# Scores, mask, scale and row maximum: one VectorE operation per head in place of two per half of the heads

## The chip, the cores and the metric

The kernel runs on one core of one Trainium2 chip. Its engines work side by side, each through its own list of instructions in order: TensorE (PE in the profile, with PEld for its weight loads), VectorE (DVE), ScalarE (ACT), GpSimd (POOL) and SyncE (SP), which here issues nearly all DMAs. The metric is the device time of one execution in microseconds. Three runs of the kernel before gave 841.65, 842.85 and 843.45; the median is 842.85.

## The reference

Eight sequences of 576 tokens with eight heads of 64 pass through a causal attention with a window of 64 tokens, and then through a mixer with a token step and a channel step:

```python
scores = scale * np.matmul(q, k.transpose(0, 1, 3, 2))
rel = pos[:, None] - pos[None, :]
mask = (rel >= 0) & (rel < window)
scores = np.where(mask, scores, -1000000000.0)
scores = scores - np.max(scores, axis=-1, keepdims=True)
attn = np.exp(scores)
attn = attn / (np.sum(attn, axis=-1, keepdims=True) + 1e-09)
x = np.matmul(attn, v)                                  # then heads side by side: [8, 576, 512]
u = x + (np.maximum(xt @ w_tok1, 0.0) @ w_tok2).T       # xt is x with tokens last
out = u + np.maximum(u @ w_ch1, 0.0) @ w_ch2
```

All inputs are float32 but the mixer's weights, which arrive as float64 and are converted on the chip. Matrix products of the mixer use each operand as a high and a low part (hi, lo) and three products.

## The kernel before

**Tiles.** The tokens of each sequence are nine blocks of 64. An attention tile is two such blocks, 128 rows of queries, and there are 36 of them, i = 0 to 35. Since the window is 64 tokens, a block of 64 queries meets 128 keys: its own block and the one before. So the scores of a tile are, for each of the eight heads, 128 rows by 128 keys. The heads come in two halves, u = 0 and u = 1 (head g = 2h + u, h = 0 to 3), and each half has one PSUM buffer of 128 x 512, called s, written by `qk` (L295).

**Softmax.** `softmax(i, u)` works on one half. For tiles 0 to 6 (N_PE is 7) the mask has been added by TensorE, and VectorE reduces the maximum straight from PSUM (L309, L310). For tiles 7 to 35 VectorE first multiplies the scores by the scale and adds the mask over the whole half, 512 elements, into a tile e in SBUF (L312), and then reduces e to the negated maximum of each of the four heads, four columns of the tile nm (L315). `softmax_exp` then takes the exponential of each head on ScalarE with that column as its bias, and sums it at the same time (L323, two instructions in the profile).

**After the softmax.** `pt_transpose` turns e on TensorE (L330, tile pp) and ScalarE copies it back (L332, pt). `av` multiplies with the values (L342, tile xp). `recip` adds 1e-9 to the sums and inverts them on VectorE (L350, L351, tile ri), and `norm` multiplies xp with that into x (L356). `split_x` makes the high part on ScalarE (L101, xhi) and the low part on GpSimd (L104, xlo). `tok1` (L387) multiplies xhi and xlo into h, `finish_h` and `finish_h_low` apply the ReLU and split it (L398, L407), and `tok2` makes one piece of u at a time: x is transposed into the PSUM tile up (L428), the second token product is added (L435), and ScalarE copies it out (L440).

**Conversion jobs.** Between these steps the float64 weights are converted on VectorE: `to_f32_a` (L204, L206, L207) and `to_f32_b` (L216, L218, L219), then an addition on GpSimd (L221), a copy on ScalarE and a subtraction on GpSimd (L101, L104). Whether a tile has such a job is written in the table JOBS.

**Order.** The order of each engine's instructions is the order in which the program calls these functions; nothing reorders it. One turn i of the loop (L497) gives, for the stage from tile 7 on: the transposes of tile i; `softmax(i + 1, 0)`; `recip(i)`; finished weight jobs and `split_x`; `softmax_exp(i + 1, 0)`; one piece of u; the first part of a conversion; `softmax(i + 1, 1)`; `tok1`; `softmax_exp(i + 1, 1)`; the second part of the conversion; `av(i)` and `norm`; the ReLU's low part; `qk(i + 2)`; and another piece of u. The score buffers have two slots, so `qk(i + 2)` needs the buffers of tile i + 1, which `softmax(i + 1, u)` frees. The tile e has four slots, nm three.

**Masks.** At the start GpSimd fills two masks of 128 x 128 (L168 to L173) with 0 and NEG, and ScalarE writes a second form of each, maskr, for the TensorE path, multiplied to NEG_PE (L174).

After the attention stage come the channel products (L651, L659, L871), which the change does not touch.

Of the kernel before, what the change touches and what calls it, by code (L numbers as in the profile page):

```python
# [15 lines left out]
AF = mybir.ActivationFunctionType  # L16
ALU = mybir.AluOpType
AX = mybir.AxisListType
# [4 lines left out]
P = 128  # L23
# [24 lines left out]
N_PE, N_EARLY = 7, 4  # L48
# [9 lines left out]

HOME = {"m1": "c2", "m6": "c3", "m7": "c4", "m5": "c5", "m2": "c6", "m4": "c0", "m3": "c1"}
SLOT, NSLOT = NPROD * 2 * P, 3  # L60
NEG = -1.0e9

NEG_PE = -2.0 ** 33

F64_LOW = 2.0 ** -15
F64_HIGH = struct.unpack("<f", struct.pack("<I", 0x47EFFFFF))[0]
# [7 lines left out]
def tile_blocks(i):  # L74

    p, t = divmod(i, TPP)
    if t == 4:
        return (2 * p, 8), (2 * p + 1, 8)
    b, t = (2 * p, t) if t < 4 else (2 * p + 1, t - 5)
    return (b, t), (b, t + 4)  # L80
# [3 lines left out]
def mixer_kernel(ctx: ExitStack, tc: tile.TileContext, qh, kh, vh, wt1, wt2, wc1, wc2, out):  # L84
    nc = tc.nc
    scale = 1.0 / math.sqrt(D)
# [36 lines left out]
    with ExitStack() as actx:  # L123
# [4 lines left out]
        mask = [pa.tile([P, P], F32, name=f"mask{m}") for m in range(2)]  # L128
# [21 lines left out]
        maskr = [pa.tile([P, P], F32R, name=f"maskr{m}") for m in range(2)]  # L150
# [13 lines left out]
        for m in (1, 0):  # L164
            nc.gpsimd.memset(mask[m], 0.0)
            for half in range(2):
                mh = mask[m][half * BLK:(half + 1) * BLK]
                nc.gpsimd.affine_select(out=mh, in_=mh, compare_op=ALU.is_ge, fill=NEG,  # L168
                                        base=-1, pattern=[[1, P]], channel_multiplier=-1)
                nc.gpsimd.affine_select(out=mh, in_=mh, compare_op=ALU.is_ge, fill=NEG,  # L170
                                        base=BLK, pattern=[[-1, P]], channel_multiplier=1)
            if m == 1:
                nc.gpsimd.memset(mask[1][0:BLK, 0:BLK], NEG)  # L173
            nc.scalar.activation(maskr[m], mask[m], AF.Copy, scale=NEG_PE / NEG)  # L174

        for c in range(2):
            nc.gpsimd.tensor_copy(swapped[:, c * BLK:(c + 1) * BLK], ident[:, (1 - c) * BLK:(2 - c) * BLK])
# [89 lines left out]
        s_ps, e_sb, st = {}, {}, {}  # L267
# [31 lines left out]
        def softmax(i, u):  # L299
            if u == 0:  # L300
                st[i] = (pa.tile([P, H], F32, name=f"nm{i}", tag="nm", bufs=3),
                         pa.tile([P, H], F32, name=f"sum{i}", tag="sum", bufs=3))
            nm, sm = st[i]
            mk = mask[1 if tile_blocks(i)[0][1] == 0 else 0]
            e = pa.tile([P, 4, P], F32, name=f"e{i}_{u}", tag="e", bufs=4)
            e_sb[i, u] = e
            nmu = nm.rearrange("p (j u) -> p j u", u=2)[:, :, u]
            if i < N_PE:
                nc.vector.tensor_reduce(out=nmu, in_=s_ps[i, u], axis=AX.X, op=ALU.max, negate=True)  # L309
                nc.vector.tensor_scalar_mul(nmu, nmu, scale)  # L310
                return
            nc.vector.scalar_tensor_tensor(  # L312
                out=e, in0=s_ps.pop((i, u)), scalar=scale,
                in1=mk.unsqueeze(1).to_broadcast([P, 4, P]), op0=ALU.mult, op1=ALU.add)
            nc.vector.tensor_reduce(out=nmu, in_=e, axis=AX.X, op=ALU.max, negate=True)  # L315

        def softmax_exp(i, u):
            e = e_sb[i, u]
            nm, sm = st[i]
            src, by = (s_ps.pop((i, u)), scale) if i < N_PE else (e, 1.0)  # L320
            for h in range(4):
                g = 2 * h + u
                nc.scalar.activation(e[:, h], src[:, h], AF.Exp, bias=nm[:, g:g + 1], scale=by,  # L323
                                     accum_out=sm[:, g:g + 1])
# [167 lines left out]
        for i in range(TOK1_FROM, NT + 1):  # L492
            m = min(n + (1 if i < TOK1_SLOW else 2), i)
# [3 lines left out]
        for i in range(-1, NT + 1):  # L497
# [18 lines left out]
            if i + 1 < NT:  # L516
                softmax(i + 1, 0)
# [11 lines left out]
            if i + 1 < NT:  # L529
                softmax_exp(i + 1, 0)  # L530
# [7 lines left out]
            if i + 1 < NT:  # L538
                softmax(i + 1, 1)
# [3 lines left out]
            if i < N_PE - 1:  # L543
                softmax_exp(i + 1, 1)
                while to_finish:
                    job_finish()
            for n in tok1_plan.get(i, ()):
                tok1(n)
            if N_PE - 1 <= i < NT - 1:
                softmax_exp(i + 1, 1)  # L550
# [29 lines left out]
    with ExitStack() as bctx:  # L580
# [89 lines left out]
        def new_op(name, ct):  # L670
            tag, bufs = OP_TAGS[ct]
            return ps.tile([P, CHUNK], F32, name=f"op{name}_{ct}", tag=tag, bufs=bufs)
# [13 lines left out]
        u = ul.pop(0)  # L686
# [12 lines left out]
        for ct in range(NCT):  # L699
# [3 lines left out]
            op = new_op("0", ct)  # L703
# [84 lines left out]
        for j in range(1, N_PLAIN):  # L788
            u, last = ul.pop(j), j == N_PLAIN - 1
# [4 lines left out]
            for half in range(2):  # L794
                g = []
# [33 lines left out]
                for ct in range(NCT):  # L829
                    op = new_op(f"{j}_{half}", ct)  # L830
# [141 lines left out]
```

## Time and profile before

| what | value |
|---|---|
| median of 3 runs | 842.85 us (841.65 to 843.45) |
| the profiled execution | 843.08 us |
| its span, first to last instruction | 841.3 us |
| mean granted TensorE clock | 0.993 |
| L312, mask and scale, 128x512 | 58 times, 39.2 us, mean 676 ns |
| L315, negated maximum, 128x512 to 128x4 | 58 times, 39.8 us, mean 686 ns |
| L323, exponential, 128x128 | 232 times, 90.5 us, mean 398 ns |

Times are microseconds unless marked ns. In a row of a group the fields are line, engine, operation, output <- input, shapes, count, then the busy time and the mean duration of one, then the idle time of the engine just before them and what ended it. In a row in order of time the first two fields are the start, counted from the start of the span, and the duration. In a waits row stand who waited, for whom, microseconds in total, times, and the longest. In a row of a stretch stand its length, the busy time and number of instructions of PE, PEld, DVE, ACT and POOL, the granted TensorE clock, the busy share of the DMA engines and GB/s.

### The profile page before, as it was taken

To read this page: it belongs to the slowest core of one execution; us is meant where nothing else is said; L and a number is where in the kernel's file an instruction comes from. 1 tells how busy PE (TensorE), PEld (TensorE's weight loads), DVE (VectorE), ACT (ScalarE), POOL (GpSimd) and SP (SyncE) were. 2 spreads that over 40 slices of the span, in tenths; PEclk is the share of its full clock that TensorE was granted. 3 is DMA by queue.
4 is the path that set the end of the run, shared out by engine and by line. 5 is a ranking of instruction groups with operands and counts; after the bars stand their busy time and mean duration, and the time that the engine had idled before them with its cause. 6 is when DMAs were issued, how large, how long until landed. Compare 5 with 4: busy or idle time off the path is not lost.

```text
span 841.3 us, 14830 instructions
## 1 busy us (share of the span) xinstructions
PE 820.7 (98%) x5878; PEld 681.4 (81%) x5878; DVE 529.1 (63%) x940; ACT 336.6 (40%) x1017; POOL 104.6 (12%) x110
## 2 busy tenths in 40 slices
PE   8989999999999999999999999999999999999998
PEld 5668888888879878888888888878888878888886
DVE  5889988888884795666425535367635367625252
ACT  6778889888885441213203211024202033202020
POOL 4433434343332000000000000000000000000000
PEclk9999999999999999999999999999999999999999
DMA  9657687677644546744413642324542424542002
GB/s 329 210 202 250 206 253 242 218 246 249 206 134 151 195 121 187 209 139 135 141 73 111 246 194 87 138 88 138 187 188 88 138 91 169 171 170 88 1 1 100
DMA packets 71621, 136.49 MB, mean 162 GB/s; under 512 B 7040, under 2 KB 41856, under 8 KB 69632
## 3 DMA queue, kind: packets, MB, share of 16 engines
q1 hardware_dynamic: 69440, 133.71, 46.8%
q10 hardware_dynamic: 2112, 1.84, 0.7%
q8 instruction: 46, 0.75, 0.4%
q14 instruction: 23, 0.19, 0.1%
HBM read 104.66 MB, written 30.87 MB: 161 GB/s over the span
## 4 chain that ended last, share of the span: by engine, by line
PE 69%; DVE 23%; issue 3%; ACT 3%; DMA 1%; SPq 0%; POOL 0%; POOLq 0%; DVEq 0%; ACTq 0%
PE gp L871 19%; PE op L659 11%; PE gp L651 8%; PE op_4a L659 4%; PE op_2b L659 4%; PE op_2a L659 4%; PE op_0b L659 4%; PE op_0a L659 4%; PE op_4b L659 4%; DVE nm L315 3%; DVE e L312 2%; PE up L435 2%; PE h L387 2%; DVE x L356 2%; DVE r L219 2%
## 5 line engine op out<-in xcount | busy, mean ns | idle before, releaser
L871 PE MATMUL gp<-m,w1hi 128*128 128x512 f32 x504 | 155.4, 389 | 0.7 <-DVE x L879 0.7
L871 PEld LDWEIGHTS gp<-m,w1hi 128*128 128x128 f32 x504 | 94.4, 188 | 21.2 <-DVE x L879 1.5
L871 PE MATMUL gp<-m,w1lo 128*128 128x512 f32 x252 | 98.1, 389 | 0.0
L323 ACT ACTIVATE e<-e,nm 128x128 f32<-128x128 f32 x232 | 90.5, 398 | 18.1 <-DVE nm L315 17.6
L638 ACT ACTIVATE ghi<-x 128x512 fp32r<-128x512 f32 x54 | 34.2, 632 | 119.9 <-DVE x L881 68.3
L875 ACT COPY x<-gp 128x512 f32<-128x512 f32 x18 | 10.4, 577 | 143.8 <-PE gp L871 143.8
L639 DVE SCALAR_TENSOR_TENSOR glo<-x,ghi 128x512 fp32r<-128x512 f32 x54 | 37.4, 693 | 38.1 <-ACT ghi L638 38.1
L638 ACT ACTIVATE ghi<-gp 128x512 fp32r<-128x512 f32 x50 | 29.8, 596 | 70.5 <-PE gp L651 70.4
L651 PE MATMUL gp<-ulo,w1hi 128*128 128x512 f32 x144 | 56.0, 389 | 0.0
L651 PE MATMUL gp<-uhi,w1hi 128*128 128x512 f32 x144 | 56.0, 389 | 0.0
L651 PE MATMUL gp<-uhi,w1lo 128*128 128x512 f32 x144 | 56.0, 389 | 0.0
L871 PEld LDWEIGHTS gp<-m,w1lo 128*128 128x128 f32 x252 | 47.3, 188 | 9.7
L342 PEld LDWEIGHTS xp<-v,pt 128*64 128x64 f32 x1152 | 38.2, 142 | 15.0 <-issue 7.0
L639 DVE SCALAR_TENSOR_TENSOR glo<-gp,ghi 128x512 fp32r<-128x512 f32 x50 | 34.4, 687 | 24.7 <-ACT ghi L638 24.6
L659 PE MATMUL op<-ghi,w2hi 128*128 128x512 f32 x128 | 49.8, 389 | 0.0
L659 PE MATMUL op<-ghi,w2lo 128*128 128x512 f32 x128 | 49.8, 389 | 0.0
L659 PE MATMUL op<-glo,w2hi 128*128 128x512 f32 x128 | 49.8, 389 | 0.0
L104 POOL TENSOR_TENSOR xlo<-x,xhi 128x512 fp32r<-128x512 f32 x32 | 41.3, 1290 | 40.3 <-ACT xhi L101 39.9
L342 PE MATMUL xp<-v,pt 128*64 128x64 f32 x1152 | 43.2, 230 | 2.1 <-ACT t1hi L101 1.9
L323 ACT ACTIVATION_READ_ACCUMULATOR e<-e,nm 128x1 f32 x232 | 45.0, 194 | 0.0
L435 PE MATMUL up<-t2hi,hhi 128*128 128x320 f32 (+1 forms) x128 | 43.0, 336 | 0.0
L330 PE MATMUL pp<-ident,e 128*128 128x128 f32 x288 | 42.2, 280 | 0.5
(168 smaller groups left out, 1888.4 us busy)
## 6 DMA issues: line engine op xcount, KB each, us to landing
v<-vh SPq DMA_DIRECT2D x36, 512.0 KB, 3.8
w1hi<-w1s SPq DMA_DIRECT2D x18, 896.0 KB, 4.5
w1lo<-w1s SPq DMA_DIRECT2D x18, 896.0 KB, 6.3
raw<-wc SPq DMA_DIRECT2D x32, 384.0 KB, 4.4
q<-qh SPq DMA_DIRECT2D x36, 256.0 KB, 4.4
k<-kh SPq DMA_DIRECT2D x7, 1280.0 KB, 8.3
out<-uf SPq DMA_DIRECT2D x35, 256.0 KB, 2.7
uf<-u_dram SPq DMA_DIRECT2D x8, 1024.0 KB, 9.1
```

The costliest lines, as they stand in the source:

```text
L104: eng_lo.tensor_sub(lo, src, hi.bitcast(F32))
L219: nc.vector.scalar_tensor_tensor(out=rf, in0=low.bitcast(U32), scalar=2.0 ** -52, in1=rf, op0=ALU.mult, op1=ALU.mult)
L315: nc.vector.tensor_reduce(out=nmu, in_=e, axis=AX.X, op=ALU.max, negate=True)
L323: nc.scalar.activation(e[:, h], src[:, h], AF.Exp, bias=nm[:, g:g + 1], scale=by, accum_out=sm[:, g:g + 1])
L330: nc.tensor.transpose(pp[:, h], e[:, h], ident)
L342: nc.tensor.matmul(xp[half * BLK:(half + 1) * BLK, h], pts[h % 2][:, h // 2, half * BLK:(half + 1) * BLK], vt[:, half, h], start=True, sto ...
L435: nc.tensor.matmul(up[:, :n], hx[:, cs], w[:, tt * S + s0:tt * S + s0 + n], start=False, stop=(k == 6), skip_group_check=True)
L638: nc.scalar.activation(hi, src, AF.Relu)
L639: nc.vector.scalar_tensor_tensor(out=lo, in0=src, scalar=0.0, in1=hi.bitcast(F32), op0=ALU.max, op1=ALU.subtract)
L651: nc.tensor.matmul(gp, w[:, w1_at(ft, ct)], x[:, ct], start=(k == 0), stop=(k == 3 * NCT - 1))
L659: nc.tensor.matmul(op, w[:, ct, ft], x[:, cols], start=(first and k == 0), stop=(last and k == 3 * len(gs) - 1), skip_group_check=not (fir ...
L871: nc.tensor.matmul(b, w[:, at], c[:, h, t], start=(n < 4 and k == 0), stop=(k == 5), skip_group_check=True)
```

## The change

For tiles 7 to 35, `softmax` no longer works on a half with two operations. For each of the four heads it issues one `tensor_tensor_reduce` on VectorE over 128 elements. It reads the scores from PSUM and the mask, writes (scores + mask) x (-scale) into e, and writes the minimum of these, which is the negated maximum of the scaled scores, into one column of nm. Since e now holds the negated scores, `softmax_exp` passes a scale of -1 in place of 1 for these tiles. As the mask is now added before the scaling, its fill is -2^33 instead of -1e9 for both masks, and the form for TensorE becomes a plain copy.

```diff
-NEG = -1.0e9
-
-NEG_PE = -2.0 ** 33
+
+NEG = -2.0 ** 33
+MAX_F32 = 3.0e38
...
-            nc.scalar.activation(maskr[m], mask[m], AF.Copy, scale=NEG_PE / NEG)
+            nc.scalar.copy(maskr[m], mask[m])
...
-            nc.vector.scalar_tensor_tensor(
-                out=e, in0=s_ps.pop((i, u)), scalar=scale,
-                in1=mk.unsqueeze(1).to_broadcast([P, 4, P]), op0=ALU.mult, op1=ALU.add)
-            nc.vector.tensor_reduce(out=nmu, in_=e, axis=AX.X, op=ALU.max, negate=True)
+
+            s = s_ps.pop((i, u))
+            for h in range(4):
+                g = 2 * h + u
+                nc.vector.tensor_tensor_reduce(out=e[:, h], in0=s[:, h], in1=mk, scale=-scale, scalar=MAX_F32,
+                                               op0=ALU.add, op1=ALU.min, accum_out=nm[:, g:g + 1])
...
-            src, by = (s_ps.pop((i, u)), scale) if i < N_PE else (e, 1.0)
+            src, by = (s_ps.pop((i, u)), scale) if i < N_PE else (e, -1.0)
```

## The prediction

> **What bounds the kernel now.** I began with the page's busy shares and its forty slices.
>
> ```profile
> PE 820.7 (98%) x5878; PEld 681.4 (81%) x5878; DVE 529.1 (63%) x940; ACT 336.6 (40%) x1017; POOL 104.6 (12%) x110
> PE   8989999999999999999999999999999999999998
> DVE  5889988888884795666425535367635367625252
> ```
>
> TensorE is busy nearly everywhere, VectorE (DVE) only 63%. But a slice is 21 us, and from the second to the twelfth, the attention part, DVE stands at 8 or 9. The changed lines run there alone, for tiles 7 to 35, so I asked for that stretch by itself: busy time per engine, then DVE's groups, then who waited for whom.
>
> ```profile
> 55.00:255.00 200.00, 193.46 (x2690) 166.16 (x2688) 180.31 (x341) 169.33 (x637) 78.73 (x69) 1.00 0.66 216
> ```
>
> ```profile
> L315 DVE TENSOR_REDUCE nm<-e 128x4 f32<-128x512 f32 x58 | 39.8, 686 | 2.0
> L312 DVE SCALAR_TENSOR_TENSOR e<-s,mask 128x512 f32<-128x512 f32 x58 | 39.2, 676 | 1.6 <-PE s L295 1.6
> L350 DVE TENSOR_SCALAR ri<-sum 128x8 f32<-128x8 f32 x30 | 21.5, 716 | 0.0
> L356 DVE TENSOR_TENSOR x<-xp,ri 128x512 f32<-128x512 f32 x29 | 19.9, 686 | 10.8 <-PE xp L342 10.5
> ```
>
> ```profile
> ACT e L323 <- DVE nm L315: 17.6, 17, 1.4
> DVE x L356 <- PE xp L342: 10.5, 8, 1.7
> ```
>
> The first row gives, in this order, PE 193.5, weight loads 166.2, DVE 180.3, ACT 169.3 and POOL 78.7 us of 200. No engine is alone at its limit: PE shows 6.5 us idle, DVE 19.7. The 29 tiles take about 6.9 us each. The pairs L312 and L315 fill 79 us of DVE, which is the most that could be shortened. The waits row for x says that in 8 tiles DVE stood waiting for PE; in the other 21 it ran into L356 late. Those 21 are where DVE time can count.
>
> Next the chain of waits, cut to 114 to 137 us:
>
> ```profile
> by line: DVE nm L315 17.9%; DVE e L312 15.9%; DVE ri L350 11.0%; DVE x L356 10.9%; DVE c L207 7.7%; DVE r L219 7.3%; DVE c L216 6.2%; DVE hlo L407 5.2%; DVE r L218 4.9%; DVE c L206 4.8%; DVE c L204 3.1%; issue 2.9%; DVE ri L351 2.7%; PE xp
> ```
>
> Here the chain is DVE from end to end, and a third of it is the pair. Taken at its word, every microsecond saved there would count. One group makes me doubt it: L350 adds 1e-9 to 8 elements and is given 716 ns. So I read one tile in order of time, on DVE, and the one POOL row beside it.
>
> ```profile
> 122.61 0.68 DVE L356 TENSOR_TENSOR x<-xp,ri 128x512 f32<-128x512 f32 x1
> 123.21 0.68 DVE L312 SCALAR_TENSOR_TENSOR e<-s,mask 128x512 f32<-128x512 f32 x1
> 123.92 0.69 DVE L315 TENSOR_REDUCE nm<-e 128x4 f32<-128x512 f32 x1
> 124.53 0.80 DVE L350 TENSOR_SCALAR ri<-sum 128x8 f32<-128x8 f32 x1
> 125.36 0.20 DVE L351 RECIPROCAL ri<-ri 128x8 f32<-128x8 f32 x1
> 125.48 0.31 DVE L204 TENSOR_SCALAR c<-raw 128x384 int32<-128x384 int32 x1
> 126.50 0.69 DVE L312 SCALAR_TENSOR_TENSOR e<-s,mask 128x512 f32<-128x512 f32 x1
> 127.22 0.69 DVE L315 TENSOR_REDUCE nm<-e 128x4 f32<-128x512 f32 x1
> 127.82 0.55 DVE L216 SCALAR_TENSOR_TENSOR c<-raw,c 128x384 int32<-128x384 int32 x1
> 128.87 0.56 DVE L219 SCALAR_TENSOR_TENSOR r<-raw,r 128x384 f32<-128x384 uint32 x1
> 129.34 0.68 DVE L356 TENSOR_TENSOR x<-xp,ri 128x512 f32<-128x512 f32 x1
> ```
>
> ```profile
> 124.02 1.28 POOL L104 TENSOR_TENSOR xlo<-x,xhi 128x512 fp32r<-128x512 f32 x1 [0.25 <-ACT xhi L101]
> ```
>
> ```profile
> L350 DVE TENSOR_SCALAR ri<-sum x36: 154/802/1234, 13.5 to 253.1; 128x8 f32<-128x8 f32 x36
> ```
>
> L350 begins at 124.53 and ends at 125.33; POOL's xlo ends at 125.30. The same operation takes 154 ns at its shortest. It is held until POOL is done, and no semaphore shows it. POOL's start comes from x (L356) through ScalarE's xhi. So the loop that repeats is: x, xhi, xlo, end of L350, then on DVE the conversions, the pair for u=1, more conversions, x again. The pair for u=0 lies beside xhi and xlo. The mean L350 of the stage, 716 ns, less 154 says that about 0.56 us per tile is such waiting.
>
> [...]
>
> **The change part by part.** Removed: 58 L312 and 58 L315. From 123.21 to 124.53 a pair takes 1.32 us of DVE's time: 0.71 for L312, since L315 reads what it wrote and starts 0.03 after its end, and 0.61 for L315, since L350 does not need its result and starts before its end.
>
> Added: 232 operations of 128 elements, four to a half. They write different heads, so none needs another. The trace of before has none. Their step comes from two sizes: 512 elements take 0.60 (122.61 to 123.21), 384 take 0.47 (128.87 to 129.34), so 128 elements cost 0.13, and one of 128 wide takes 0.60 - 3 x 0.13 = 0.21.
>
> Beside the 128 results, each must deliver one minimum per partition. ScalarE does the like for its sums, and its rows show the price:
>
> ```profile
> 121.26 0.40 ACT L323 ACTIVATE e<-e,nm 128x128 f32<-128x128 f32 x1 [0.96 <-DVE nm L315]
> 121.57 0.19 ACT L323 ACTIVATION_READ_ACCUMULATOR e<-e,nm 128x1 f32 x1
> 121.66 0.39 ACT L323 ACTIVATE e<-e,nm 128x128 f32<-128x128 f32 x1
> ```
>
> A second instruction of one element, 0.09 us from its start to the next. DVE's nearest is the reciprocal of 8 elements, 125.36 to 125.48: 0.12. The lower end is nothing, if the minimum leaves with the operation. The upper end is that the reader waits for the operation's end: 128 elements last 0.68 - 3 x 0.13 = 0.29, then 0.03, then 0.12, in all 0.44 per head; if the next head waits for the reader's end as well, 0.29 + 0.03 + 0.20 + 0.03 = 0.55. I take a reader that overlaps, 0.09, since ScalarE's is the same kind of step: 0.30 per head, 1.20 per half, 0.12 less than 1.32.
>
> [...]
>
> For u=0 the saving is worth nothing: L350 only starts its wait earlier. Equally a u=0 half could grow by about 0.56 us on average and stay hidden; beyond that POOL's cover is gone and it counts in full. For u=1 the 0.12 counts in the 21 tiles that do not wait for xp: 21 x 0.12 = 2.5 us. Were the chain of waits taken at its word, both halves would count, 58 x 0.12 = 7.0 us; that is inside the range below.
>
> What else moves. ScalarE's first exponential can start after one head, some 0.3 us after the half begins instead of 1.50 (154.81 to 156.31 below), and the 17.6 us of its waits mostly go. I price that at nothing, because what is late next is still DVE's x, as this tile shows:
>
> ```profile
> 154.81 0.68 DVE L312 SCALAR_TENSOR_TENSOR e<-s,mask 128x512 f32<-128x512 f32 x1
> 155.40 1.24 PE L295 MATMUL s<-k,q 64*64 64x128 f32 x32
> 156.31 0.40 ACT L323 ACTIVATE e<-e,nm 128x128 f32<-128x128 f32 x1 [1.32 <-DVE nm L315]
> 157.65 0.68 DVE L356 TENSOR_TENSOR x<-xp,ri 128x512 f32<-128x512 f32 x1
> 158.37 0.62 ACT L101 CAST xhi<-x 128x512 fp32r<-128x512 f32 x1 [0.41 <-DVE x L356]
> 158.90 0.36 ACT L440 COPY u<-up 128x256 f32<-128x256 f32 x1
> 159.31 0.44 PE L428 MATMUL up<-ident,x 128*128 128x128 f32 x2 [0.72 <-ACT u L440]
> ```
>
> The exponentials waited 1.32, yet PE's only stall, 0.72 at 159.31, is for a copy queued on ScalarE behind xhi, which waited for x. An earlier x pays there. The scores' buffer is freed later: L312 let it go after 0.68, four heads after 1.20. In this tile L295, two tiles ahead, starts 0.59 after L312 and its matmuls into the u=1 buffer would wait some 0.5 more, with transposes and u pieces queued behind them on PE. Cover: the 0.72 stall in the same tile. Without that cover it would cost up to 0.5 in the tiles where DVE is this late.
>
> The masks' two ScalarE copies (L174, from a scaled activation to a copy) run before the first softmax:
>
> ```profile
> 4.63 0.31 ACT L174 ACTIVATE maskr<-mask 128x128 fp32r<-128x128 f32 x1 [1.23 <-POOL mask L170]
> 8.41 0.37 ACT L323 ACTIVATE e<-s,nm 128x128 f32<-128x128 f32 x1 [3.48 <-DVE nm L310]
> ```
>
> ScalarE idles 3.48 us after them, so their price either way is nothing; uncovered it could not pass 0.31 each. The constants and the sign in L323 cost nothing. No DMA or queue is moved.
>
> Sum: 2.5 us off. The profiled execution took 843.08 (span 841.3, 1.8 around it), 0.23 above the median of the runs; 843.08 - 2.5 = 840.6, in medians 842.85 - 2.5 = 840.35, so 840.4.
>
> **The rivals.**
>
> *The minimum leaves with the operation.* No reader: 4 x 0.21 = 0.84 per half, 0.48 less, 21 x 0.48 = 10.1 us. PE's idle of 6.5 us is a lower bound on what can be taken, because stretched matmuls count as busy. That gives 836.4 to 832.8. Against it: the reader on ScalarE. Chance 0.17.
>
> *Nothing to measure.* Each small operation pays more fixed time than the two sizes show, as with the 0.12 of the reciprocal: 4 x 0.33 = 1.32, the old price; or the next POOL operation eats the gain, as xlo does for u=0 (L204 is a tensor_scalar too). 842.9. [...] Chance 0.16.
>
> *The reader waits* (slower). Place: the u=1 half, between conversions and x. At 0.44 per head a half takes 1.76, 0.44 more; 21 x 0.44 = 9.2, u=0 hidden by POOL: 852.1. With both waits 2.20: 21 x 0.88 = 18.5, and u=0 passes its cover by 0.88 - 0.56 = 0.32 in up to 29 tiles, 9.3 more: 870.7. It decides from 0.33 per head on. For it: L312 to L315 shows that DVE does wait where a result is read. Against: ScalarE's reader starts 0.09 before its activation's end. Chance 0.25, of it 0.07 for both waits.
>
> **How the numbers follow.** The forecast, a reader that overlaps (0.28 to 0.33 per head, -4.2 to 0 us), has 0.42. What a measurement can tell from no change is 0.2%, 1.7 us, that is a half of 1.24 us or less, 0.31 per head. Of the forecast's 0.42 I give 0.31 to faster, 0.11 to same. With the first rival faster is 0.48; with most of the second, same is 0.26; the third and a remainder make slower 0.26. The range takes in the first rival's end, 832.8, and a single wait, 852.1; outside stay both waits and the extremes, some 0.12: 832 to 853. The forecast's own range is 838.7 to 842.9.
>
> **What would show it.** Right: rows of 128x128 of some 0.29 us on DVE, a second row for each minimum, four heads in 1.20; L350 still ending with POOL's xlo and its median risen from 802 to about 920; from the start of the u=1 half to L356 2.72 instead of 2.84 (126.50 to 129.34); ScalarE's wait for nm far below 17.6; PE's 0.72 shrunk. Wrong: L350 near 154 (POOL's hold was not what set the loop), DVE rows spaced over 0.33 per head, or PE idle in L295 behind the scores' buffers.

## The result and the profile after

The changed kernel takes 834.25 us (833.41 to 835.17, 4 runs) against 843.15 us for the kernel before: a ratio of 0.9895, 95% interval 0.9883 to 0.9907, or 8.9 us less. The forecast was 840.4. The direction was right and the range, 832 to 853, holds the result. The size was not: 2.5 us were forecast, and the time landed in the range of a rival, "the minimum leaves with the operation", 832.8 to 836.4. That rival had the price right and the reason wrong: it held that there is no second instruction, and there is one.

The profiled execution took 833.92 us, with a span of 832.1 us. The busy shares of its page first:

```profile
PE 817.7 (98%) x5878; PEld 680.8 (82%) x5878; DVE 510.6 (61%) x1288; ACT 335.9 (40%) x1017; POOL 104.4 (13%) x110
```

VectorE has 348 instructions more and is busy 18.5 us less. 348 is 464 added less 116 removed, so each of the 232 operations brought a second one. The groups of VectorE in the attention stage name it, and the rows in order of time of a u=1 half show how the two lie. L316, L352 and L358 are the changed kernel's lines for the new operation, the recip's addition (L350 before) and the product x (L356 before); in the other kernels further down lines are shifted again, and the tile names tell which operation a row is.

```profile
L316 DVE CUSTOM_DVE_ANT_0 e<-s,mask 128x128 f32<-128x128 f32 x232 | 52.9, 284 | 4.1 <-PE s L295 3.7
L352 DVE TENSOR_SCALAR ri<-sum 128x8 f32<-128x8 f32 x30 | 27.4, 914 | 0.0
L316 DVE DVE_READ_ACCUMULATOR2_ANT nm<- 128x1 f32 x232 | 19.2, 83 | 0.0
L216 DVE SCALAR_TENSOR_TENSOR c<-raw,c 128x384 int32<-128x384 int32 x22 | 13.5, 615 | 0.0
```

```profile
121.30 0.28 DVE L316 CUSTOM_DVE_ANT_0 e<-s,mask 128x128 f32<-128x128 f32 x1
121.51 0.08 DVE L316 DVE_READ_ACCUMULATOR2_ANT nm<- 128x1 f32 x1
121.51 0.29 DVE L316 CUSTOM_DVE_ANT_0 e<-s,mask 128x128 f32<-128x128 f32 x1
121.72 0.08 DVE L316 DVE_READ_ACCUMULATOR2_ANT nm<- 128x1 f32 x1
...
122.14 0.86 DVE L216 SCALAR_TENSOR_TENSOR c<-raw,c 128x384 int32<-128x384 int32 x1
...
123.98 0.68 DVE L358 TENSOR_TENSOR x<-xp,ri 128x512 f32<-128x512 f32 x1
```

The reader is there, 83 ns long, but it starts in the same moment as the next head's operation (121.51 and 121.51). From head to head it is 0.21 us, and from the first head to the next other operation 0.84 (121.30 to 122.14), where the old pair took 1.32. By the groups, the recip's addition is now longer, a mean of 914 ns against 716: that is the u=0 half's saving, or a part of it, turned into waiting for GpSimd.

What became of the stage is told by the busy time of PE, weight loads, DVE, ACT and POOL between 55 and 247 us, and by what the chain of waits holds between 110 and 133 us:

```profile
55.00:247.00 192.00, 191.61 (x2692) 166.23 (x2690) 162.55 (x684) 168.60 (x636) 77.95 (x69) 1.00 0.68 226
```

```profile
by line: PE h L389 22.0%; PE up L437 20.1%; PE xp L344 14.1%; PE s L295 13.5%; PE up L430 9.6%; PE pp L332 8.5%; ACT e L325 6.7%; ACT xhi L101 2.2%; ACT hhi L400 2.1%; ACT u L442 1.4%; issue 0.2%
```

TensorE is busy for 191.6 of 192 us, and the chain, which was VectorE from end to end, is nearly all TensorE. The waits that paid are TensorE's. In the kernel before, these three rows are the whole list of what TensorE's matmuls (PE; the weight loads have a list of their own) waited for between 55 and 255 us:

```profile
PE up L428 <- ACT u L440: 4.8, 7, 1.1
PE h L387 <- POOL xlo L104: 1.2, 2, 0.8
PE h L387 <- DVE hlo L407: 1.2, 1, 1.2
```

In the changed kernel the same list, between 55 and 247 us, is empty. One of these waits was the 0.72 us at 159.31, for a copy behind xhi. The same tile in the changed kernel:

```profile
152.50 0.62 ACT L101 CAST xhi<-x 128x512 fp32r<-128x512 f32 x1 [0.98 <-DVE x L358]
153.02 0.37 ACT L442 COPY u<-up 128x256 f32<-128x256 f32 x1
153.44 0.44 PE L430 MATMUL up<-ident,x 128*128 128x128 f32 x2
```

The transpose at 153.44 follows at once. And VectorE now waits for TensorE more than before, in 12 tiles instead of 8 (waits between 55 and 247 us):

```profile
DVE x L358 <- PE xp L344: 19.9, 12, 3.2
```

### The profile page after: what moved, and what is told of

Its sections match the earlier page's. It is cut to its first block, busy times and chain, and to the rows that moved or that the text cites. A ratio compares the mean times of both kernels' runs of the same rounds, so it can differ in the third digit from the quotient of the medians.

```text
span 832.1 us, 15193 instructions
## 1 busy us (share of the span) xinstructions
PE 817.7 (98%) x5878; PEld 680.8 (82%) x5878; DVE 510.6 (61%) x1288; ACT 335.9 (40%) x1017; POOL 104.4 (13%) x110
## 4 chain that ended last, share of the span: by engine, by line
PE 83%; DVE 9%; ACT 4%; issue 2%; DMA 1%; POOL 0%; POOLq 0%; DVEq 0%; ACTq 0%; SPq 0%
PE gp L873 19%; PE op L661 11%; PE gp L653 8%; PE up L437 5%; PE h L389 5%; PE op_2a L661 4%; PE op_0a L661 4%; PE op_4a L661 4%; PE op_0b L661 4%; PE op_2b L661 4%; PE op_4b L661 4%; PE s L295 3%; PE xp L344 3%; PE pp L332 3%; PE up L430 2%
## 5 line engine op out<-in xcount | busy, mean ns | idle before, releaser
L316 DVE CUSTOM_DVE_ANT_0 e<-s,mask 128x128 f32<-128x128 f32 x232 | 52.9, 284 | 4.1 <-PE s L295 3.7
L344 PEld LDWEIGHTS xp<-v,pt 128*64 128x64 f32 x1152 | 37.5, 140 | 15.1 <-ACT e L325 10.1
```

The lines of the kernel that those rows point to most:

```text
L316: nc.vector.tensor_tensor_reduce(out=e[:, h], in0=s[:, h], in1=mk, scale=-scale, scalar=MAX_F32, op0=ALU.add, op1=ALU.min, accum_out=nm[:, ...
L344: nc.tensor.matmul(xp[half * BLK:(half + 1) * BLK, h], pts[h % 2][:, h // 2, half * BLK:(half + 1) * BLK], vt[:, half, h], start=True, sto ...
```

## The experiments

Theory A is the prediction's loop: x, ScalarE's xhi, GpSimd's xlo, the end of the held addition, the conversions and the u=1 half, x again; the u=0 half lies beside xlo. Rival B says that the gain comes from ScalarE, which may start an exponential after one head instead of four. Rival C says that VectorE's time counts wherever it is. Each ratio below is against the kernel before on the same chip (medians of 842.94 to 843.27 us).

**One half alone.** In both kernels the other half keeps the old pair, and its exponentials the scale of 1 (that line is left out here):

```diff
+            if u != 0:      # e1_u0_only; u != 1 in e2_u1_only
+                nc.vector.scalar_tensor_tensor(
+                    out=e, in0=s, scalar=scale,
+                    in1=mk.unsqueeze(1).to_broadcast([P, 4, P]), op0=ALU.mult, op1=ALU.add)
+                nc.vector.tensor_reduce(out=nmu, in_=e, axis=AX.X, op=ALU.max, negate=True)
+                return
```

> The new operation in the u=0 half alone; the u=1 half keeps the two old ones. Theory A (the loop through x, xhi, GpSimd's xlo and the held L350; u=0 lies beside xlo): no change, 842 to 843.5 us, and the recip's addition stands longer by about 0.48 us per tile. Rival B (ScalarE may start a head's exponential earlier, and that made the gain): about half of it, 838 to 839.5 us. Rival C (all VectorE time counts alike): also half, 838 to 839.5 us.

> The new operation in the u=1 half alone. Theory A: nearly the whole gain, 834 to 835.5 us. Rivals B and C: about half, 838 to 839.5 us.

Measured: u=0 alone 840.97 us, ratio 0.9972 (0.9962 to 0.9981); u=1 alone 835.25 us, ratio 0.9907 (0.9893 to 0.9920). So the u=1 half brings 7.8 us and the u=0 half 2.1. B and C, which treat the halves alike, are out. A is right about where most of it is, but its "nothing" for u=0 is wrong by 2.1 us.

The group of the recip's addition with u=0 alone shows where a part of that half's saving went, into waiting for GpSimd: 927 ns against 716, that is 6.3 us over 30 additions, and 0.21 us per tile where 0.48 was expected.

```profile
L358 DVE TENSOR_SCALAR ri<-sum 128x8 f32<-128x8 f32 x30 | 27.8, 927 | 0.0
```

The half saved 29 x 0.48 = 13.9 us of VectorE's time. Besides the 6.3 us and the 2.1, L206 is held more (mean 587 to 693 ns, 2.2 us in 21 operations), and VectorE waits longer for TensorE's xp (10.5 to 14.3 us).

**VectorE's time put back.** An operation with no use, a reduction of 384 constants, behind the four heads of one half, of both, or of the u=0 half when only that is changed (fill is a tile of 128 x 2):

```diff
+            if u == 1:      # e3_fill_u1; u == 0 in e4_fill_u0 and e11; no condition in e12_fill_both
+                nc.vector.tensor_reduce(out=fill, in_=zero[:, :192].unsqueeze(1).to_broadcast([P, 2, 192]),
+                                        axis=AX.X, op=ALU.max)
```

> The changed kernel with one idle VectorE operation more after the four heads of each u=1 half, a reduction over 384 elements of a constant whose result nobody reads, about 0.47 us: VectorE's time in that half is the old 1.32 us, while ScalarE may still start after the first head. Theory A: the gain is given back, 841 to 843.5 us. Rival B: it stays, 834 to 835 us. Rival C: about half is left, 838 to 839.5 us.

> The same idle VectorE operation, after the u=0 half instead. Theory A: no change, 834 to 835 us, and the addition of the recip is held for some 0.47 us less. Rival C: half of the gain is lost, 838 to 839.5 us. Rival B: 834 to 835 us.

> The new operation in the u=0 half alone, with the idle VectorE operation of 0.47 us behind it, so that this half takes VectorE the old 1.31 us. It asks where the 2.1 us come from that the u=0 half brought by itself. If from VectorE's time, in the tiles whose L350 is not held: 842 to 843.5 us. If from ScalarE's earlier exponentials: 840.5 to 841.5 us.

> The changed kernel with the idle operation of 0.47 us behind both halves: VectorE's time is the old one everywhere, and all that is left of the change is that heads are done one by one. Theory A: 841.5 to 843.5 us. If the earlier exponentials are worth something by themselves: 839.5 to 841.5 us, like with the filler in the u=1 half alone.

The filler's row and the next, with the filler in u=1:

```profile
127.36 0.55 DVE L320 TENSOR_REDUCE fill<-zero 128x2 f32<-128x384 f32 x1
127.83 0.55 DVE L217 SCALAR_TENSOR_TENSOR c<-raw,c 128x384 int32<-128x384 int32 x1
```

It takes 0.47 (127.36 to 127.83). Measured: behind u=1 840.03 us (0.9967, 0.9955 to 0.9979); behind u=0 834.87 (0.9908, 0.9895 to 0.9922); behind both 842.16 (0.9990, 0.9981 to 0.9999); u=0 alone with its filler 842.72 (0.9995, 0.9987 to 1.0004).

With the filler behind u=1 alone no forecast was met: 3.0 us stay, less than C's half and more than A's nothing. That is near the 2.1 us that the u=0 half, still short in this run, brings by itself.

With the filler behind both halves VectorE's time is the old one and the exponentials may still start after one head: ScalarE's waits for nm fall from 17.6 us to 1.4. Yet only 1.1 us is left (0.1 to 1.6 by the interval): that bounds what B can claim. The u=0 half alone with its filler says where that half's 2.1 us came from: with its time put back they are gone, so it was VectorE's time there too.

How VectorE's time ahead of xlo can count is seen in one tile, first in the kernel before, then with u=0 alone, each with GpSimd's row (POOL):

```profile
117.28 1.28 POOL L104 TENSOR_TENSOR xlo<-x,xhi 128x512 fp32r<-128x512 f32 x1 [3.71 <-ACT xhi L101]
117.46 1.13 DVE L350 TENSOR_SCALAR ri<-sum 128x8 f32<-128x8 f32 x1
...
118.75 0.31 DVE L204 TENSOR_SCALAR c<-raw 128x384 int32<-128x384 int32 x1
119.09 0.36 DVE L206 TENSOR_SCALAR c<-c 128x384 f32<-128x384 f32 x1
```

```profile
117.64 0.17 DVE L358 TENSOR_SCALAR ri<-sum 128x8 f32<-128x8 f32 x1
...
117.95 1.47 POOL L104 TENSOR_TENSOR xlo<-x,xhi 128x512 fp32r<-128x512 f32 x1 [3.70 <-ACT xhi L101]
117.96 0.31 DVE L204 TENSOR_SCALAR c<-raw 128x384 int32<-128x384 int32 x1
118.31 1.33 DVE L206 TENSOR_SCALAR c<-c 128x384 f32<-128x384 f32 x1
```

Before, the addition starts behind xlo's start and is held, and L204 and L206 come behind the hold. With u=0 shortened the addition starts 0.31 ahead of xlo, it and L204 are done early, and L206 is held in their place, so less is left to do behind the hold. In the kernel before, the addition stands free ahead of xlo in one tile of the stage; with u=0 alone it does so in five, and in four of these the next tensor_scalar, L204 or L206, is held over 1.2 us instead. That these tiles make up the 2.1 us is likely; their shares were not measured one by one.

The filler in u=0 of the changed kernel, in contrast, costs little: 8.2 us of gain are left, against 8.9 without it, and the intervals of the two overlap. It takes 29 x 0.47 = 13.6 us, but the addition's mean falls from 914 to 618 ns (8.9 us in all) and L206's from 549 to 407 (3.0 us): most of it was spent inside the holds.

```profile
L356 DVE TENSOR_SCALAR ri<-sum 128x8 f32<-128x8 f32 x30 | 18.5, 618 | 0.0
```

**The heads in reverse.** ScalarE takes head 0 first, which now comes last:

```diff
-            for h in range(4):
+            for h in reversed(range(4)):
```

> The changed kernel with the four heads of a half done in the order 3, 2, 1, 0, so that ScalarE's first exponential (head 0) waits for all four; VectorE's time is the same. Theory A (VectorE's time in the u=1 half): no change, 834 to 835.5 us. Rival B (the earlier exponential): a good part of the gain is lost, 837 us or more.

Measured: 834.60 us, ratio 0.9899 (0.9886 to 0.9912), the changed kernel's own. B is out a second time.

**The second half moved, in the kernel before and in the changed one.** No VectorE work is saved; `softmax(i + 1, 1)` is called right behind the u=0 call:

```diff
             if i + 1 < NT:
                 softmax(i + 1, 0)
+            if N_PE <= i + 1 < NT:
+                softmax(i + 1, 1)
...
-            if i + 1 < NT:
+            if i + 1 < N_PE:
                 softmax(i + 1, 1)
```

> The kernel before, both old operations kept, with the u=1 half's mask, scale and maximum moved up to stand right behind the u=0 half's, ahead of the recip and of the first part of the conversion. No VectorE work is saved. Theory A (the loop runs through GpSimd's xlo, beside which VectorE has time to spare): the second pair now lies beside xlo as well, the addition of the recip is hardly held any more, and most of the gain appears without the new operation, 833 to 837 us. Rival C (VectorE's total time): no change, 842 to 844 us.

> The same move in the changed kernel. TensorE was busy 191.6 of 192 us of the stage in the changed kernel, so by theory A, which now has TensorE as the bound, nothing is left to gain: 833 to 835 us. If VectorE's loop still sets the pace in part, 830 to 833 us.

Measured: the kernel before with the move 836.22 us, ratio 0.9922 (0.9908 to 0.9937), so 6.7 us of the gain came without the new operation. Rows of VectorE and GpSimd in that kernel:

```profile
119.76 0.69 DVE L312 SCALAR_TENSOR_TENSOR e<-s,mask 128x512 f32<-128x512 f32 x1 [0.33 <-PE s L295]
...
121.80 0.69 DVE L315 TENSOR_REDUCE nm<-e 128x4 f32<-128x512 f32 x1
122.41 0.16 DVE L350 TENSOR_SCALAR ri<-sum 128x8 f32<-128x8 f32 x1
...
123.07 1.06 DVE L206 TENSOR_SCALAR c<-c 128x384 f32<-128x384 f32 x1
```

```profile
120.16 1.28 POOL L104 TENSOR_TENSOR xlo<-x,xhi 128x512 fp32r<-128x512 f32 x1 [0.64 <-ACT xhi L101]
122.90 1.01 POOL L104 TENSOR_TENSOR w1lo<-w,w1hi 128x384 fp32r<-128x384 f32 x1 [1.46 <-ACT w1hi L101]
```

The two pairs run from 119.76 on, across xlo, which ends at 121.44 while the second is under way, and the addition behind them is free, 0.16. In this tile L206 meets GpSimd's next operation, w1lo, and ends only at 124.13. That is no loss of the move over the whole stage: L206's mean is 474 ns here and 587 in the kernel before, where w1lo holds L206 or L207 in eight tiles.

The changed kernel with the move takes 833.53 us, ratio 0.9887 (0.9874 to 0.9900). Its interval covers the changed kernel's 0.9895, so no further gain is measured. The addition's mean falls from 914 to 266 ns, and VectorE's waits for xp rise from 19.9 to 30.4 us (between 55 and 247 us): the time that is freed becomes waiting for TensorE, which is the bound by now.

**The recip without its addition.** The kernel before, in which `recip` inverts the sums as they are; the addition of 1e-9 is left out:

```diff
-            nc.vector.tensor_scalar_add(ri, sm, 1e-9)
-            nc.vector.reciprocal(ri, ri)
+            nc.vector.reciprocal(ri, sm)
```

> The kernel before without the recip's addition of 1e-9 (L350), which is left out. [...] If L350 itself was the slow one, its 17 us of waiting go from VectorE and the time falls like with the changed kernel, 833 to 836 us.

Measured: 837.03 us, ratio 0.9928 (0.9914 to 0.9942), above the 833 to 836 forecast for a slow addition. VectorE's group, and a tile's rows on VectorE and GpSimd:

```profile
L204 DVE TENSOR_SCALAR c<-raw 128x384 int32<-128x384 int32 x21 | 16.5, 784 | 0.0
```

```profile
121.73 0.19 DVE L350 RECIPROCAL ri<-sum 128x8 f32<-128x8 f32 x1
121.84 0.65 DVE L204 TENSOR_SCALAR c<-raw 128x384 int32<-128x384 int32 x1
122.52 0.36 DVE L206 TENSOR_SCALAR c<-c 128x384 f32<-128x384 f32 x1
```

```profile
120.98 1.28 POOL L104 TENSOR_TENSOR xlo<-x,xhi 128x512 fp32r<-128x512 f32 x1 [0.25 <-ACT xhi L101]
```

The addition itself was not the slow one: the hold moved on to L204 (its mean 784 ns; 353 before). By itself that would leave the time as it was, and it fell, by the loop: what stands behind the hold had become shorter. In the kernel before, xlo ended at 125.30, and behind it came the end of L350, then L351 and L204, and only then L206, 0.53 later:

```profile
125.83 0.36 DVE L206 TENSOR_SCALAR c<-c 128x384 f32<-128x384 f32 x1
```

Now the reciprocal is done ahead of the end, and L206 starts 0.26 after it (122.26 to 122.52). An estimate from this one tile, 0.27 us in 21 tiles, gives 5.7 us; 6.2 were measured. The agreement may be partly luck, since other holds changed as well: L206's mean fell from 587 to 407 ns. Freeing the held operation and shortening what follows it cannot be told apart by this run.

**The reader's price.** Four more of the operations ahead of each u=0 half, without the minimum:

```diff
+            if u == 0:
+                for h in range(4):
+                    nc.vector._custom_dve(bass._DVE_TTR_OPS[ALU.add, ALU.min], out=e[:, h], in0=s[:, h], in1=mk,
+                                          s0=MAX_F32, s1=-scale)
```

> The changed kernel with four more operations ahead of each u=0 half, of the same kind but without the minimum's output, writing what the real ones then overwrite. It prices the reader: if the reader lies fully beside the next head's operation, the step from one of these to the next is 0.21 us as with a reader; if the reader takes time of its own, it is shorter by it, 0.13 to 0.15 us. The time stays within 834 to 837 us, since the u=0 half lies beside xlo up to about 2.1 us.

Measured: 835.10 us in one run. The first row below is the four without a reader, merged; the rows behind it are the first two real ones.

```profile
125.24 0.88 DVE L316 CUSTOM_DVE_ANT_0 e<-s,mask 128x128 f32<-128x128 f32 x4 [0.16 <-PE s L295]
126.04 0.28 DVE L320 CUSTOM_DVE_ANT_0 e<-s,mask 128x128 f32<-128x128 f32 x1
126.25 0.08 DVE L320 DVE_READ_ACCUMULATOR2_ANT nm<- 128x1 f32 x1
126.25 0.28 DVE L320 CUSTOM_DVE_ANT_0 e<-s,mask 128x128 f32<-128x128 f32 x1
```

Four steps without a reader take 0.80 (125.24 to 126.04), 0.20 each; with a reader the step is 0.21. By these rows the reader costs 0.01 us, the last digit that they show.

## Why the prediction was right in direction and wrong in size

- *The step of the new operation, 0.21 by extrapolation from 512 and 384 elements.* Right: 0.20 without a reader, and a duration of 0.284 where 0.29 was expected. Four of 128 elements without a reader take 0.80, where the one of 512 from which the step was worked out, L356, took 0.60.
- *A reader per head, 0.09.* It exists, 232 times, but its price is 0.01. This is the term that was mis-sized. ScalarE's reader was taken as the nearest row, and the 0.09 was the time from its start to the next activation, not what the step would have been without a reader, which no row showed. VectorE's reader starts together with the next operation. A half takes 0.84 instead of 1.20, and its saving is 0.48 instead of 0.12.
- *The saving counts for the u=1 half in 21 tiles.* The half is shown by the halves and the fillers; that it is these 21 tiles was not measured. The size that follows from the measured step is 21 x 0.48 = 10.1 us; 7.8 were measured with u=1 alone. TensorE's idle time, 6.5 us, was the lower bound given with that rival, and stretched matmuls do show: 2690 of them were busy 193.5 us in the kernel before, 2692 in the changed one 191.6. With u=1 alone TensorE was busy 194.2 of 195 us (55 to 250), and VectorE's waits for xp rose from 10.5 to 20.4 us: TensorE had become the bound. The holds that the sum left out moved both ways: L216 met GpSimd's w1lo (mean 548 to 598 ns), while L206 was held less (587 to 408). How the missing 2.3 us split was not measured.
- *The u=0 half is worth nothing.* Nearly: 2.1 us by itself, and about 1 us or less on top of the u=1 half (8.9 us saved with both, 7.8 with u=1 alone, 8.2 with the filler in u=0; the intervals overlap). The mean wait of 0.56 us per tile, which the prediction used as cover, hid that the cover ends where the addition starts ahead of xlo.
- *ScalarE's earlier exponentials are worth nothing.* Right within 1.1 us: reversed heads 834.60, fillers in both halves 842.16. Their waits of 17.6 us did vanish, as expected, and paid next to nothing.
- *The scores' buffers and the mask copies.* The later release of the buffer shows no cost: the list of TensorE's waits in the stage is empty. The mask copies still end (4.93 us) ahead of the first softmax (its first operation, L309, starts at 8.39), and the kernel with u=0 alone and its filler, which has the new ones too, takes the time of the kernel before within its interval (0.9987 to 1.0004).
- *The slower rival* did not come about: the next operation on VectorE did not wait for the reader's end (both start at 121.51, the reader lasts 0.08).
- *The signs.* Two came out near the forecast by luck. From the start of the u=1 half to x the tile shown takes 2.68 (121.30 to 123.98), where 2.72 was forecast and 2.84 stood before; but the half saved 0.48 there and L216, held, gave 0.31 back. The addition's median is 910 ns, where about 920 was forecast from a saving a quarter as large; with u=0 alone many additions take 1.28.

## What to carry to other kernels

Before a saving on an engine is counted, look for operations there that are far longer than the same operation elsewhere in the trace: they can hide a wait that no semaphore shows (here the addition, 716 ns in the mean and 154 at its shortest). Work ahead of such a hold was nearly free here (2.1 us of 13.9), and work behind it counted (7.8 us) until another engine became the bound. An operation that escapes the hold can pass it on to the next one (L204, 353 to 784 ns in the mean). A price for an unseen instruction that is taken from another engine should leave both ends in the sum; here the truth lay at the low end, beside an overlap that the engine's own rows showed for independent operations (0.68 long, 0.60 from one to the next). A chain of waits follows the instruction before when no releaser is shown, so it can name work that lies beside the real path.

## What the runs showed of the hardware

- The VectorE operation that also delivers a minimum per partition was two instructions, 232 of each, and the second (83 ns) ran beside the next one: 0.21 us from head to head with it, 0.20 without.
- GpSimd's 1.28 us subtraction (xlo) held the VectorE tensor_scalar in SBUF that came next: the 8-element addition (0.16 alone, up to 1.29), L204 (353 to 784 ns in the mean when the addition is left out) or L206 (0.36 alone, 1.33 at 118.31 with u=0 alone). In the kernel before, 28 of the 30 additions between 55 and 255 us ended 0.02 to 0.04 after the GpSimd operation beside them. The 1.01 us one (w1lo) did the same to L206 (1.06 at 123.07 in the kernel before with the move). Without the addition, the reciprocal beside xlo was not held, 0.19 at 121.73 and 193 ns in the mean of 30, though it has one input in SBUF like the addition: the number of inputs alone does not tell which of these operations is held. No semaphore shows the hold.
- An operation with two inputs in SBUF was touched too: L216 took 0.86 us at 122.14 beside GpSimd's w1lo (121.57 to 122.59), against a longest of 558 ns in the kernel before:

```profile
121.57 1.02 POOL L104 TENSOR_TENSOR w1lo<-w,w1hi 128x384 fp32r<-128x384 f32 x1 [1.47 <-ACT w1hi L101]
```
